# Attention with an exponential feature map, then a gated FFN: the numerator of batch 0 scaled inside its PSUM bank and divided from there on VectorE, in a new order of the whole program

## The chip, the cores and the metric

The kernel runs on one core of a Trainium2 chip. The metric is the device time of one execution in microseconds (us), measured from outside the program; each figure below is a median of several executions, or one execution taken with the hardware profiler.

The engines are named as the profile names them: PE is TensorE's matmuls and PEld its weight loads, DVE is VectorE, ACT is ScalarE, POOL is GpSimd, SP is SyncE, which only issues transfers here.

## The reference

```python
batch, n_heads, seq, head_dim, d_feat = 8, 8, 576, 64, 128
n_tokens, d_model, d_ff = 4608, 512, 1536

def phi(x):
    proj = einsum('bhsd,df->bhsf', x, w_phi)
    proj = proj - max(abs(proj), axis=-1, keepdims=True)
    return concatenate([exp(proj), exp(-proj)], axis=-1)

q_p, k_p = phi(q), phi(k)
kv  = einsum('bhsf,bhsd->bhfd', k_p, v)
z   = sum(k_p, axis=2)
num = einsum('bhsf,bhfd->bhsd', q_p, kv)
den = einsum('bhsf,bhf->bhs', q_p, z)[..., None] + 1e-06
x   = (num / den).transpose(0, 2, 1, 3).reshape(4608, 512)
out = (maximum(x @ w_gate, 0) * (x @ w_val)) @ w_out
```

So for each batch and head there is a sum over tokens (kv, with z as one more column), then for each token a numerator and a denominator, then a division. Behind the attention stands a feed-forward network (FFN) over all 4608 tokens.

## The kernel before

**Tiles.** A batch's 576 tokens are split into 512 (four tiles of 128) and 64. The 512 go through the FFN with their batch, as groups 0 to 7; the 64 of each batch are collected into a ninth group, number 8. PSUM is used as eight banks of 128 x 512 float32, which every step names itself.

**The order.** The whole program is a list of words, the string ORDER: some thousands of steps, each written as `name.arguments:banks@buffers`. A loop at the end of the kernel calls the function `do_<name>` for each word in turn, and so every engine gets its instructions in the order of the list. Nothing else schedules. An instruction waits where the data it reads, the bank that it writes or the buffer that it reuses isn't free yet, and everything behind it on its engine waits too.

**The attention of a batch.** `k3`, `k0` and their like project k with w_phi (L668, L592); `ke` takes exponentials of the projection into kp on ScalarE (L688); `kx` takes the maxima on VectorE (L696); `kk` makes factors from these; `vs`, `vq` and `vo` multiply v by the factors, mostly on GpSimd; `kv` sums over the tokens (L794), and `kc` or `kd` copies the sum out of PSUM, on ScalarE or VectorE. For q, `qe` takes exponentials into qp (L869), `qx`, `qy`, `qz` and `qu` find the maxima, and `qw` makes from them cq, the factor exp(2 max) of a token and head (L910).

**The numerator.** For each token the feature map has two halves, s = 0 and s = 1; their maximum is taken out of the exponent by scaling half 1 with cq, and the rest cancels in the division. The eight heads are dealt into three banks (GROUPS = 2, 3 and 3 heads). For each tile i of 128 tokens and each group g of heads:

- `nu` (L917, TensorE): for each head two matmuls, half 0 and half 1, side by side in the bank, 65 columns each (64 of the numerator and, as the last, the denominator).
- `nt` (L938, VectorE): t = half 1 x cq, from PSUM to a buffer; 130 or 195 elements in a row.
- `nv` (L948, VectorE): u = half 0 + t, from PSUM and the buffer.
- once for the tile, `nr` (L956, VectorE): r = 1 / (denominator), eight numbers in a row.
- once for the tile, `nx` (L960, GpSimd): xu = u x r, 512 elements in a row, to bfloat16.

```python
nc.vector.tensor_tensor(t_of(3 * serial(b, i) + g)[:, 0:n], parts(bk, n)[:, :, 1],          # nt
    scales(b, i)[:, lo:hi][:, :, None].to_broadcast([P, n, E]), op=ALU.mult)
nc.vector.tensor_tensor(u_of(serial(b, i))[:, lo:hi], parts(bk, n)[:, :, 0],                # nv
    t_of(3 * serial(b, i) + g)[:, 0:n], op=ALU.add)
nc.vector.reciprocal(r_of(serial(b, i)), u_of(serial(b, i))[:, :, D : D + 1])               # nr
eng.tensor_tensor(xu_of(n).rearrange("p (h d) -> p h d", d=D), u_of(n)[:, :, 0:D],          # nx
    r_of(n).to_broadcast([P, H, D]), op=ALU.mult)
```

xu must be transposed before the FFN. In batch 0 this is done by TensorE (`xp`, L997, into PSUM) and a copy on ScalarE (`xa`, L1011) or VectorE (`xc`, L1005); in the other batches by a transposing DMA (`xt`).

**The FFN.** Group 0 is computed in pieces of 128 tokens by four slices of the hidden layer (`pv` and `pg`, L1224: 16 matmuls of 128 columns each). Groups 1 to 6 take a hidden slice of 128 for all 512 tokens (`fv` and `fg`, L1097: four matmuls of 512 columns). The product x @ w_val is copied out of PSUM as val, by ScalarE (`va`, L1112; `pa` in group 0) or VectorE (`vb`, L1115); then VectorE takes relu(gate) x val in one instruction (`ga`, L1118). The multiplication by w_out (`fw`, L1361) uses seven products of half-size blocks instead of eight; their sums of inputs are made on GpSimd (`ps`, L1337). Groups 7 and 8 are paired in a similar scheme (`fi`, L1194).

**Dummies.** `zz.n` issues n matmuls on a tile of zeros (L455), whose results nobody reads; there are 85 in all, nearly all of them before the first FFN matmul.

## Time and profile before

| | |
|---|---|
| time, median of 3 runs | 360.83 us (359.58, 360.83, 360.85) |
| the profiled execution's own time | 360.87 us |
| its span in the profile | 359.1 us |
| instructions in the profile | 10076 |
| first FFN matmul of group 0 (L1224) starts | 28.67 us |
| matmuls on zeros (L455) | 85 |
| nt (L938) with cq, 64 of 195 and 32 of 130 elements, busy | 21.8 + 8.9 us |
| nv (L948), 72 of 195 and 36 of 130 elements, busy | 24.3 + 9.9 us |
| nx (L960) on GpSimd, 36, busy | 37.4 us |

The profile is one execution, taken by the hardware profiler. Its span runs from the first to the last instruction, and the execution's own time lies 1.8 us above it. A row such as `L938 DVE TENSOR_TENSOR t<-bank,cq 128x195 f32<-128x195 f32 x64 | 21.8, 348 | ...` is a group of instructions: line of the code, engine, operation, what is written from what, the shapes and types, how many; then the busy time in us and the mean of one in ns; then the idle time of the engine just ahead of them and what ended it. A row of the timeline has the start in us, the busy time in us, the engine, and the instructions that follow each other there. The names of buffers stand without their numbers.

### The profile page before, as it was taken

The page shows a single profiled execution, that of the slowest core. Times are in us where ns is not written, and L with a number is a line of the kernel's source. Part 1 is how long each engine was busy: PE and PEld are TensorE (multiplying, and loading weights), DVE is VectorE, ACT ScalarE, POOL GpSimd, SP SyncE. Part 2 cuts the span into 40 slices and gives each one's busy share as a digit, 9 for nine tenths or more (in the row PEclk, how much of TensorE's full clock was granted, in tenths as well). Part 3 has the DMA queues.
Part 4 walks back from the last instruction along what each step waited for, and adds up shares of the span by engine and source line. Part 5 has one row for each costly group of instructions (what it writes and reads, how often), then busy time and mean ns, then how long its engine had stood idle before and what let it go on. Part 6 is the DMA issues. An engine that isn't in the chain of part 4 may idle for free.

```text
span 359.1 us, 10076 instructions
## 1 busy us (share of the span) xinstructions
PE 352.9 (98%) x3876; PEld 222.2 (62%) x3876; DVE 312.9 (87%) x721; ACT 235.8 (66%) x564; POOL 325.6 (91%) x393
## 2 busy tenths in 40 slices
PE   8999999999999999999999999999999999999996
PEld 6678966445575656765576546666656566444684
DVE  5999999989999999999997999999898853898744
ACT  3999996986698869786897269656861424454310
POOL 8674988999999999976999589989999999999994
PEclk9999999999999999999999999999999999999999
DMA  7999999990947494369215980778300221600017
GB/s 124 257 198 204 164 199 159 180 164 7 178 68 157 53 157 95 68 127 135 58 39 105 158 136 2 176 107 103 62 0 16 45 59 25 227 0 2 0 31 206
DMA packets 90770, 38.16 MB, mean 106 GB/s; under 512 B 64226, under 2 KB 86370, under 8 KB 90722
## 3 DMA queue, kind: packets, MB, share of 16 engines
q0 software_dynamic: 33504, 15.03, 32.5%
q1 hardware_dynamic: 56754, 21.83, 27.7%
q10 hardware_dynamic: 464, 0.66, 0.8%
q8 instruction: 30, 0.49, 0.6%
q14 instruction: 18, 0.15, 0.1%
HBM read 37.81 MB, written 9.44 MB: 132 GB/s over the span
## 4 chain that ended last, share of the span: by engine, by line
PE 85%; DVE 8%; ACT 2%; DMA 2%; issue 1%; POOL 1%; SPq 0%; DVEq 0%
PE bank L1097 35%; PE bank L1361 18%; PE bank L1194 10%; PE bank L794 5%; PE bank L1224 4%; PE bank L917 3%; PE bank L592 2%; PE bank L854 2%; PE bank L1256 2%; ACT kp L688 2%; DMA w64f<-in_w_phi_dram 2%; DVE t L938 1%; DVE u L948 1%; DVE h L1118 1%; DVE mk L696 1%
## 5 line engine op out<-in xcount | busy, mean ns | idle before, releaser
L688 ACT ACTIVATE kp<-bank 128x384 bf16<-128x384 f32 x192 | 84.2, 513 | 16.6 <-DVE mk L696 7.4
L1097 PE MATMUL bank<-xTs,wv 128*128 128x512 bf16 x304 | 75.7, 379 | 0.0
L1097 PE MATMUL bank<-xTs,wg 128*128 128x512 bf16 x304 | 74.6, 379 | 0.0
L869 ACT ACTIVATE qp<-bank 128x512 bf16<-128x512 f32 x128 | 69.9, 627 | 6.5 <-PE bank L854 4.2
L1118 DVE SCALAR_TENSOR_TENSOR h<-bank,val 128x512 bf16<-128x512 f32 x90 | 60.5, 680 | 6.7 <-PE bank L1097 4.5
L1112 ACT CAST val<-bank 128x512 bf16<-128x512 f32 x59 | 35.1, 594 | 33.4 <-PE bank L1097 30.4
L745 POOL TENSOR_TENSOR vs<-vn,ek 128x780 bf16<-128x780 f32 (+2 forms) x40 | 53.8, 1366 | 0.8 <-ACT ek L705 0.4
L696 DVE TENSOR_REDUCE mk<-bank 128x3 f32<-128x384 f32 x96 | 49.1, 542 | 0.2
L960 POOL TENSOR_TENSOR xu<-u,r 128x512 bf16<-128x512 f32 x36 | 37.4, 1045 | 11.6 <-DVE r L956 11.5
L1361 PEld LDWEIGHTS <-h 128*128 128x128 bf16 x432 | 41.1, 98 | 10.0 <-issue 2.6
L1097 PEld LDWEIGHTS <-wg 128*128 128x128 bf16 x304 | 27.8, 98 | 30.2 <-issue 1.3
L1097 PEld LDWEIGHTS <-wv 128*128 128x128 bf16 x304 | 27.6, 98 | 27.3 <-issue 0.9
L877 DVE TRANSPOSE_TENSOR_REDUCE maxq<-bank 128x16 f32<-128x512 f32 x56 | 36.9, 690 | 0.1
L948 DVE TENSOR_TENSOR u<-bank,t 128x195 f32<-128x195 f32 (+1 forms) x108 | 32.9, 327 | 1.8 <-POOL xu L960 0.9
L1361 PE MATMUL bank<-wo,h 128*128 128x256 bf16 x260 | 32.5, 273 | 0.0
L1337 POOL TENSOR_TENSOR vs<-h 128x256 bf16<-128x256 bf16 x42 | 28.0, 671 | 3.7 <-DVE h L1118 3.6
L938 DVE TENSOR_TENSOR t<-bank,cq 128x195 f32<-128x195 f32 (+1 forms) x96 | 29.6, 326 | 1.9 <-PE bank L917 1.2
L917 PEld LDWEIGHTS <-qp 128*128 128x128 bf16 x512 | 23.1, 98 | 10.2 <-issue 0.5
L1337 POOL TENSOR_TENSOR h<-h,vs 128x256 bf16<-128x256 bf16 x44 | 28.6, 676 | 0.0
L1337 POOL TENSOR_TENSOR vs<-vs,h 128x256 bf16<-128x256 bf16 x42 | 28.0, 672 | 0.6
L1337 POOL TENSOR_TENSOR h<-h 128x256 bf16<-128x256 bf16 x42 | 27.9, 674 | 0.3
L917 PE MATMUL bank<-kv,qp 128*128 128x65 bf16 x512 | 26.0, 193 | 0.2 <-ACT kv L805 0.2
(156 smaller groups left out, 686.0 us busy)
## 6 DMA issues: line engine op xcount, KB each, us to landing
vn<-in_v_dram SPq DMA_DIRECT2D x24, 256.0 KB, 4.3
out_dram<-xTs SPq DMA_DIRECT2D x17, 256.0 KB, 3.0
kn<-in_k_dram POOLq DMA_DIRECT2D x7, 512.0 KB, 8.1
qn<-in_q_dram POOLq DMA_DIRECT2D x7, 512.0 KB, 8.0
out_dram<-obp SPq DMA_DIRECT2D x14, 256.0 KB, 2.6
wv<-in_moe_w_val_dram POOLq DMA_DIRECT2D x3, 512.0 KB, 9.4
wg<-in_moe_w_gate_dram POOLq DMA_DIRECT2D x3, 512.0 KB, 8.8
wo<-in_moe_w_out_dram POOLq DMA_DIRECT2D x3, 512.0 KB, 8.3
```

Source lines behind the costliest of these rows:

```text
L688: nc.scalar.activation(kp_of(3 * b + j)[:, i, s].rearrange("p n f -> p (n f)"), bank[bk[0]][:, 0 : 3 * F], AF.Exp, scale=(1.0, -1.0)[s],)
L696: nc.vector.tensor_reduce(mk_of(3 * b + j)[:, :, i], bank[bk[0]][:, 0 : 3 * F].rearrange("p (n f) -> p n f", f=F), axis=AX.X, op=ALU.max, ...
L745: nc.gpsimd.tensor_tensor(vs_of(3 * b + j)[:, s, 0:n].rearrange("p n i e -> p (n i) e")[:, :, 0:e], src[:, lo:hi].rearrange("p h i e -> p ...
L869: nc.scalar.activation(qp_of(4 * b + i)[:, s, 4 * hq : 4 * hq + 4].rearrange("p h m -> p (h m)"), bank[bk[0]], AF.Exp, scale=(1.0, -1.0)[s],)
L877: nc.vector.tensor_reduce((maxq0[:, i] if b == 0 else maxq)[:, :, i, 4 * hq : 4 * hq + 4].rearrange("p t h -> p h t"), bank[bk[0]].rearran ...
L917: nc.tensor.matmul(bank[bk[0]][:, E * n : E * (n + 1)], lhsT=qp_of(4 * b + i)[:, s, h, :], rhs=kv_of(b)[:, h, s, 0:E],)
L948: nc.vector.tensor_tensor(u_of(serial(b, i))[:, lo:hi], parts(bk, n)[:, :, 0], t_of(3 * serial(b, i) + g)[:, 0:n], op=ALU.add,)
L960: eng.tensor_tensor(xu_of(n).rearrange("p (h d) -> p h d", d=D), u_of(n)[:, :, 0:D], r_of(n).to_broadcast([P, H, D]), op=ALU.mult,)
L1097: nc.tensor.matmul(bank[bk[0]], lhsT=w[:, dc, P * f : P * f + P], rhs=xT(g)[:, dc, :], start=(dc == 0), stop=(dc == NDC - 1),)
L1118: nc.vector.scalar_tensor_tensor(h2_of(g, f), bank[bk[0]], 0.0, val_of(NFC * g + f), op0=ALU.max, op1=ALU.mult)
L1337: eng.tensor_tensor(sum_of(g, n, j), a, b, op=op)
L1361: nc.tensor.matmul(bank[bk[0]][:, col : col + HN], lhsT=x[:, P * u : P * (u + 1)], rhs=w, start=(n in (1, 5, 6) and u == us[0] and j == 0) ...
```

## The change

For the four tiles of batch 0 the steps `nu`, `nt`, `nv`, `nr` and `nx` are replaced by four new ones. The heads are dealt into two banks of four (HALVES), and each bank holds 260 columns in a row:

- `bu.0.i.g.s` (TensorE): four matmuls of 65 columns, one for each head of half g, for one half s of the features. Half s = 1 is computed first and starts the bank; s = 0 is added to it later by accumulation in PSUM.
- `bt.0.i.g` (VectorE), between the two: the bank's 260 columns are multiplied by cq in place.
- `br.0.i.g` (VectorE): reciprocals of the four denominators, read from the bank.
- `bx.0.i.g` (VectorE): xu = bank x r, 256 elements in a row, read from the bank.

12 `nu`, 12 `nt`, 12 `nv`, 4 `nr` and 4 `nx` go, and 16 `bu`, 8 `bt`, 8 `br` and 8 `bx` come; the 64 matmuls are the same in number and size. The other batches keep the old steps. Four more steps go from VectorE to ScalarE as copies of val (59 become 63, 17 become 13), and the last transposed tile of batch 0 is copied by ScalarE (`xa.0.3` for `xc.0.3`); of the copies of kv, two go over to VectorE and two to ScalarE.

ORDER is written anew from the first line to the last, with other banks and buffers. The transfers keep nearly their order. The dummies remain 85 in all. The functions that the diff adds beside these (`do_bm`, `do_fa`, `do_fb`, `do_yq`, `do_zq`, `do_z2`, `do_yr`, `do_zr`, `do_y5`, `do_y6`) are called by no word of ORDER, and `SEEDED` is empty, so that `do_fw` computes what it did.

The diff, cut to its core (two lines stand for the table ORDER, once of before and once of after):

```diff
 ORDER = """
...
-wl.1.1 kc.0.1:4 nu.0.0.0:1 nt.0.0.0:1@t0 zz.1:0 nu.0.0.2:5 qw.0.1 qx.0.1.2:2 qe.0.0.2.0:6
+bu.0.0.0.1:6 bu.0.0.1.1:7 qz.0.3:0@my2 bt.0.0.0:6 qy.0.2:2 qz.0.2:2@my0 bu.0.1.1.1:1 bu.0.1.0.1:0
...
 """
...
+    HALVES = ((0, 4), (4, 8))
...
+    def do_bu(bk, b, i, g, s):
+        lo, hi = HALVES[g]
+        for h in range(lo, hi):
+            n = h - lo
+            nc.tensor.matmul(
+                bank[bk[0]][:, E * n : E * (n + 1)],
+                lhsT=qp_of(4 * b + i)[:, s, h, :],
+                rhs=kv_of(b)[:, h, s, 0:E],
+                start=(s == 1 and h == lo),
+                stop=(h == hi - 1),
+                skip_group_check=(s == 0),
+            )
+
+    def part(bk, g):
+        lo, hi = HALVES[g]
+        return bank[bk[0]][:, 0 : E * (hi - lo)].rearrange("p (h e) -> p h e", e=E)
+
+    def do_bt(bk, b, i, g):
+        lo, hi = HALVES[g]
+        nc.vector.tensor_tensor(
+            part(bk, g),
+            part(bk, g),
+            scales(b, i)[:, lo:hi][:, :, None].to_broadcast([P, hi - lo, E]),
+            op=ALU.mult,
+        )
+
+    def do_br(bk, b, i, g):
+        lo, hi = HALVES[g]
+        nc.vector.reciprocal(r_of(serial(b, i))[:, lo:hi], part(bk, g)[:, :, D : D + 1])
+
+    def do_bx(bk, b, i, g):
+        n, (lo, hi) = serial(b, i), HALVES[g]
+        nc.vector.tensor_tensor(
+            xu_of(n).rearrange("p (h d) -> p h d", d=D)[:, lo:hi],
+            part(bk, g)[:, :, 0:D],
+            r_of(n)[:, lo:hi].to_broadcast([P, hi - lo, D]),
+            op=ALU.mult,
+        )
+
...
+    SEEDED = ()
+        firsts = (1, 5) if g in SEEDED else (1, 5, 6)
-                    start=(n in (1, 5, 6) and u == us[0] and j == 0),
+                    start=(n in firsts and u == us[0] and j == 0),
-                    skip_group_check=(n in (2, 3, 4, 7)),
+                    skip_group_check=(n not in firsts),
```

One line is added above most of the code, so a step that stood at L917 stands at L918 in the changed kernel, and those behind the new functions stand 40 lines lower and more.

What this makes of the order is seen on three engines. First TensorE's queue at the start of the program, behind the two groups of transposes of k (xTm, L645), before the change. bank_63 to bank_70 are the eight banks, `zero` is the tile of the dummies, kT the transposed k, w the projection's weights; the rows of the two dummies shown stand six times there:

```order
L645 MATMUL bank_65<-identf,xTm 128x128 x3
L455 LDWEIGHTS zero
L455 MATMUL bank_66<-zero 128x256
...
L668 LDWEIGHTS kT_77
L668 MATMUL bank_67<-w_155,kT_77 128x128
L668 LDWEIGHTS kT_77
L668 MATMUL bank_68<-w_155,kT_77 128x128
...
L410 LDWEIGHTS sel
L410 MATMUL bank_69<-w_155,sel 128x128
```

The same place after the change; the row with bank_66 stands six times, that with bank_67 four times, bank_68 once and bank_69 twice:

```order
L646 MATMUL bank_65<-identf,xTm 128x128 x3
L456 LDWEIGHTS zero
L456 MATMUL bank_66<-zero 128x256
...
L456 MATMUL bank_67<-zero 128x256
...
L456 MATMUL bank_68<-zero 128x256
L456 LDWEIGHTS zero
L456 MATMUL bank_69<-zero 128x256
...
L669 LDWEIGHTS kT_77
L669 MATMUL bank_70<-w_155,kT_77 128x128
L669 LDWEIGHTS kT_77
L669 MATMUL bank_63<-w_155,kT_77 128x128
```

Seven more dummies stand ahead of the first projection (13 for 6), and the small matmuls of L410 have left this place.

Second, VectorE's queue where the first two tiles of batch 0 are made, before the change (h, my and mz belong to the maxima of q):

```order
L938 TENSOR_TENSOR t_123<-bank_64,cq_115 128x130
L877 TENSOR_REDUCE h_152<-bank_65 128x4x4
L948 TENSOR_TENSOR u_127<-bank_64,t_123 128x130
L938 TENSOR_TENSOR t_124<-bank_63,cq_115 128x195
L938 TENSOR_TENSOR t_125<-bank_68,cq_115 128x195
L948 TENSOR_TENSOR u_127<-bank_63,t_124 128x195
L948 TENSOR_TENSOR u_127<-bank_68,t_125 128x195
L938 TENSOR_TENSOR t_126<-bank_69,cq_115 128x130
L956 RECIPROCAL r_130<-u_127 128x8
```

The same place after the change:

```order
L1008 TENSOR_TENSOR bank_69<-bank_69,cq_115 128x260
L896 TENSOR_REDUCE my_117<-bank_65 128x32
L1008 TENSOR_TENSOR bank_63<-bank_63,cq_115 128x260
L1008 TENSOR_TENSOR bank_64<-bank_64,cq_115 128x260
L904 STREAM_TRANSPOSE mz_122<-my_117 128x32
L1008 TENSOR_TENSOR bank_70<-bank_70,cq_115 128x260
L1017 RECIPROCAL r_130<-bank_64 128x4
L1017 RECIPROCAL r_131<-bank_69 128x4
L1017 RECIPROCAL r_130<-bank_63 128x4
L1021 TENSOR_TENSOR xu_133<-bank_64,r_130 128x256
L1021 TENSOR_TENSOR xu_133<-bank_63,r_130 128x256
```

The first tile's division has come over from GpSimd and stands here, behind the scalings of two tiles.

Third, ScalarE's queue up to the first copy of a transposed tile (xTs), before the change:

```order
L869 ACTIVATE qp_113<-bank_65 128x512
L869 ACTIVATE qp_112<-bank_70 128x512
L910 ACTIVATE cq_115<-mz_122 128x8
L688 ACTIVATE kp_84<-bank_68 128x384
L1011 COPY xTs<-bank_70 128x4x128
```

and after it:

```order
L870 ACTIVATE qp_113<-bank_66 128x512
L870 ACTIVATE qp_112<-bank_67 128x512
L911 ACTIVATE cq_115<-mz_122 128x8
L689 ACTIVATE kp_84<-bank_66 128x384 x2
L1051 COPY xTs<-bank_63 128x4x128
L1051 COPY xTs<-bank_69 128x4x128
```

Two exponentials of the next batch's k, for one, stand ahead of that copy, and the second tile's copy follows at once.

567 lines of the change are left out of this document (303 added, 264 removed).

## The prediction

> **What bounds the kernel now.** I read the page first, then the chain of waits, then TensorE's own waits, and then the busy time by stage, because a share over the whole span mixes stages with different limits.
>
> ```profile
> PE 352.9 (98%) x3876; PEld 222.2 (62%) x3876; DVE 312.9 (87%) x721; ACT 235.8 (66%) x564; POOL 325.6 (91%) x393
> ...
> PE 85%; DVE 8%; ACT 2%; DMA 2%; issue 1%; POOL 1%; SPq 0%; DVEq 0%
> PE bank L455 <- DVE zero L441: 1.1, 1, 1.1
> PE bank L1361 <- POOL vs L1337: 0.4, 2, 0.2
> ```
>
> TensorE is busy for 98% of the span, holds 85% of the chain that ended last, and in its list of waits hardly anything exceeds 0.2 us. So the kernel ends when TensorE has got through its queue, and a change helps only where TensorE idles or runs dummy matmuls (L455, 85 of them, which multiply zeros). The stages say which engine is beside it:
>
> ```profile
> 7.00:28.00 21.00, 20.41 (x292) 14.07 (x292) 20.71 (x54) 20.25 (x54) 15.19 (x17) 1.00 1.28 218
> 28.00:60.00 32.00, 31.80 (x532) 24.71 (x532) 31.66 (x79) 28.71 (x73) 25.43 (x30) 1.00 1.21 182
> 60.00:76.00 16.00, 15.95 (x163) 7.52 (x162) 15.94 (x41) 14.98 (x40) 15.76 (x14) 1.00 1.33 190
> 242.00:300.00 58.00, 57.58 (x561) 35.93 (x560) 46.22 (x105) 28.28 (x67) 56.92 (x71) 1.00 0.28 48
> 300.00:355.50 55.50, 55.50 (x352) 34.00 (x350) 39.24 (x63) 20.45 (x37) 53.77 (x70) 1.00 0.22 64
> ```
>
> The columns are the stretch, its length, then PE, PEld, DVE, ACT, POOL. From 7 to 76 us VectorE is busy 68.31 of 69.00 us: it never rests. From 7 to 28 ScalarE hardly rests either (20.25 of 21.00). From 242 us on VectorE has room, and GpSimd is the one that is nearly full. So there are three stages: a head (to 28.67 us) in which VectorE and ScalarE prepare batch 0 and TensorE fills time with dummies; a stretch to 76 us in which TensorE and VectorE are both full; and the rest, TensorE with GpSimd close behind. The change sits in the first stage.
>
> **How the head ends.** This is the path to the first real FFN matmul, at 28.67 us:
>
> ```profile
> 26.23 0.18 DVE L956 RECIPROCAL r<-u 128x8 f32<-128x8 f32 x1
> ...
> 26.51 1.03 POOL L960 TENSOR_TENSOR xu<-u,r 128x512 bf16<-128x512 f32 x1 [2.51 <-DVE r L956]
> ...
> 27.60 0.40 PE L997 MATMUL bank<-ident,xu 128*128 128x128 bf16 x4
> ...
> 28.03 0.59 ACT L1011 COPY xTs<-bank 128x512 bf16<-128x512 bf16 x1 [0.16 <-PE bank L997]
> ...
> 28.67 1.00 PE L1224 MATMUL bank<-xTs,wv 128*128 128x128 bf16 x15 [0.20 <-ACT xTs L1011]
> ```
>
> Reciprocal, GpSimd's division, transpose, ScalarE's copy, FFN. Before 28.67 lie all dummies; behind it TensorE is full. So the end of the program moves by as much as this point moves, plus or minus what TensorE idles later.
>
> **The numerator itself.**
>
> ```profile
> L938 DVE TENSOR_TENSOR t<-bank,cq 128x195 f32<-128x195 f32 x64 | 21.8, 348 | 1.6 <-PE bank L917 1.1 <-ACT cq L910 0.3
> L938 DVE TENSOR_TENSOR t<-bank,cq 128x130 f32<-128x130 f32 x32 | 8.9, 282 | 0.3 <-PE bank L917 0.2
> L948 DVE TENSOR_TENSOR u<-bank,t 128x195 f32<-128x195 f32 x72 | 24.3, 352 | 0.7
> L948 DVE TENSOR_TENSOR u<-bank,t 128x130 f32<-128x130 f32 x36 | 9.9, 278 | 1.1 <-POOL xu L960 0.9
> L956 DVE RECIPROCAL r<-u 128x8 f32<-128x8 f32 x36 | 6.7, 189 | 0.2
> L960 POOL TENSOR_TENSOR xu<-u,r 128x512 bf16<-128x512 f32 x36 | 37.4, 1045 | 11.6 <-DVE r L956 11.5
> L1392 DVE TENSOR_TENSOR xTs<-bank,xTs 128x256 f32<-128x256 f32 x4 | 1.7, 424 | 0.5 <-PE bank L1361 0.2
> L1216 DVE TENSOR_TENSOR val<-bank,u 128x512 bf16<-128x512 f32 x24 | 15.8, 684 | 4.6 <-PE bank L1194 3.4 <-ACT u L1210 1.2
> L1005 DVE COPY xTs<-bank 128x512 bf16<-128x512 bf16 x1 | 0.4, 384 | 0.0
> L1115 DVE CAST val<-bank 128x512 bf16<-128x512 f32 x17 | 11.4, 677 | 1.6 <-PE bank L1097 1.6
> ```
>
> Removed on VectorE, for four tiles: 8 x (348 + 352) + 4 x (282 + 278) + 4 x 189 = 8.6 us. Removed on GpSimd: 4 x 1045 = 4.2 us. Added on VectorE: 8 scalings of 260 elements in place, 8 reciprocals of 4, 8 divisions of 256. From 130 to 195 elements the row grows by 66 ns, so 260 come to 348 + 66 = 414 ns; the division is like the 256-wide row, 424; the reciprocal stays at 189. That is 8 x 1027 = 8.2 us. **VectorE saves only 0.4 us**: the addition goes to TensorE's accumulation, but the division comes over from GpSimd. No row shows a VectorE operation from PSUM to PSUM. Its bounds are the 130-wide row (282) and the 512-wide one (684), thus 8.2 - 1.1 and 8.2 + 2.2 us; I take 414, by the nearest rows. TensorE's work is unchanged: 64 matmuls of 65 columns either way, and 85 dummies either way. The old division leaves nothing late on GpSimd, which was idle 2.51 us before it.
>
> [...]
>
> Two other moves take work from VectorE in the full stretch: the last transposed tile is copied by ScalarE (384 ns less), and of the val copies two leave it and one joins before 76 us (677 ns less). With the numerator that is 0.4 + 0.4 + 0.7 = 1.5 us of VectorE's 68.3.
>
> **The start is later.** The rows of the new order show 13 dummies, not 6, between the two first transposes and the first projection.
>
> ```profile
> 1.06 3.38 PE L455 MATMUL bank<-zero 128*128 128x256 bf16 x15 [1.06 <-DVE zero L441]
> 4.23 1.49 PE L645 MATMUL bank<-identf,xTm 128*128 128x128 f32 x6
> 5.51 1.49 PE L455 MATMUL bank<-zero 128*128 128x256 bf16 x6
> 7.10 0.34 PE L668 MATMUL bank<-w,kT 64*128 64x128 bf16 x6
> 7.46 0.49 ACT L688 ACTIVATE kp<-bank 128x384 bf16<-128x384 f32 x1 [1.86 <-PE bank L668]
> 8.06 0.50 PE L455 MATMUL bank<-zero 128*128 128x256 bf16 x3
> 8.40 0.50 PE L614 MATMUL bank<-ident,kn 128*128 128x128 bf16 x6
> 11.56 1.92 ACT kp L688 x5
> ```
>
> A dummy takes (4.23 - 1.06) / 15 = 0.21 us at first and (8.40 - 8.06) / 3 = 0.11 us at 8 us, so TensorE doubles its pace in between. Six from 5.51 end at 6.8; seven more end at 7.6 (at 0.11) to 8.3 (at 0.21). The projection, at 7.10 now, then starts at 7.6 or later. ScalarE's first exponential, 0.36 us behind its projection now, moreover reads the second projection (0.1 to 0.2 us on), so it starts near 8.2 rather than 7.46. ScalarE then has the same queue up to the first copy plus one exponential (26, not 25; 1.92 / 5 = 0.38 us). With nothing gained inside, the copy would fall 0.74 + 0.38 = 1.1 us later; the old queue has some 0.3 us of idle to give. **I take +0.8 us for the first FFN matmul** (bounds 0, if VectorE's shorter path through the division and a better packing eat it up, and +1.7, if the dummies all run slowly).
>
> [...]
>
> **What comes back later.** (a) In the stretch to 76 us VectorE holds TensorE up only in fractions. Of the 1.5 us less I count 0.5 us as a gain (bounds 0 and 1.5). (b) Between operations on the whole array and those on 32-row strips TensorE loses a moment:
>
> ```profile
> 127.13 1.03 PE L1097 MATMUL bank<-xTs,wv 128*128 128x512 bf16 x4
> 128.00 0.34 PE L917 MATMUL bank<-kv,qp 128*128 128x65 bf16 x6
> 129.17 1.03 PE L1097 MATMUL bank<-xTs,wg 128*128 128x512 bf16 x4
> 130.12 0.52 PE L592 MATMUL bank<-w,kT 32*128 32x128 bf16 x24
> ```
>
> Four FFN matmuls take 0.87 us before an ordinary group, 0.95 before a strip group. The new order has 50 such changes, the old one 55: 5 x 0.08 = 0.4 us (bounds 0 and 0.5). (c) Near the end TensorE waits for GpSimd's sums:
>
> ```profile
> 290.56 1.16 POOL L1169 TENSOR_TENSOR qT<-xTs 128x512 bf16<-128x512 bf16 x1 [0.68 <-DMA xTs<-xu]
> 292.40 1.48 PE L1361 MATMUL bank<-wo,vs 128*128 128x256 bf16 x12 [0.22 <-POOL vs L1337]
> 295.39 0.83 PE L1361 MATMUL bank<-kp,vs 128*128 128x256 bf16 x6 [0.20 <-POOL vs L1337]
> ```
>
> Behind 290.56 GpSimd does not stop again, and ends 1.4 us before TensorE. It has 4.2 us less to do, but 83 rather than 82 operations behind this place, so I credit these two waits, 0.4 us (bounds 0.8 gained, 0.6 lost). (d) Two dummies now stand in the second stage, inside a time when TensorE is full: 0.1 us lost (0 to 0.2).
>
> **Sum.** The profiled execution took 360.87 us, 359.1 of it span; the median of the three runs is 360.83, the same. +0.8 - 0.5 - 0.4 - 0.4 + 0.1 = -0.4, so **360.4 us** with rounding. A measurement of this kernel can tell about 0.5%, 1.8 us, from no change: below 359.0 is faster, over 362.6 slower.
>
> **Rivals.** *Faster*: VectorE, not TensorE, sets the pace from 7 to 76 us. Then its 1.5 us count in full, and with the GpSimd waits (0.8) and the strip changes (0.5), and a head that is no later, the time is 360.87 - 2.8 = 358.1. For it: 68.31 of 69.00 us busy. Against it: TensorE is just as full from 28 us on. *Slower*: the in-place scaling costs 684 ns, not 414, in the stage in which VectorE has no rest: 8 x 0.27 = 2.2 us, thus 360.4 + 2.2 = 362.6, and with the dummies at the slow pace (another 0.5 or more) 363.2. It decides from about 680 ns. Against it: every row here grows by about 1 ns per element, whatever it reads. *No effect*: the change removes waiting that TensorE doesn't have; the order merely deals the same work out anew, 360.9. For it: 85% of the chain is TensorE, and its work is equal.
>
> **Chances.** Forecast 0.45, no effect 0.13, faster 0.24, slower 0.18. The first two lie within 0.5%. The range, 358.4 to 362.9, takes in nearly all of the faster and the slower case, the likeliest alone being 359.4 to 361.6.
>
> **What would show it.** Right: first FFN matmul near 29.5 us, the first exponential near 8.2, the scaling near 0.41 us, no wait of TensorE over 0.3 us behind 30 us, GpSimd not waiting for VectorE's reciprocal in the head. Wrong: a first FFN matmul before 28.5 us, scalings over 0.6 us, or TensorE idle for over 1 us in all behind 30 us.

## The result, and the profile after

The changed kernel takes **368.73 us** (median of 4 runs, 368.45 to 369.26), the kernel before 360.25 us beside it: a ratio of **1.0232** (95% interval 1.0217 to 1.0248). That is slower by 8.4 us, and outside the range of the prediction. The profiled execution took 368.56 us, its span 366.8 us; that of before took 360.87 and 359.1.

First the page of the changed kernel, the busy time and the chain of work that ended last:

```profile
PE 353.4 (96%) x3876; PEld 223.5 (61%) x3876; DVE 313.9 (86%) x712; ACT 237.7 (65%) x569; POOL 320.7 (87%) x389
PE 70%; POOL 8%; DVE 7%; ACT 6%; DMA 4%; issue 3%; SPq 1%; POOLq 0%; DVEq 0%; ACTq 0%
```

TensorE was 85% of the chain and is 70%; GpSimd, which was 1%, is 8%. TensorE's waits in the changed kernel (what waits, for whom; us in all, times, the longest) show where a good part of that went:

```profile
PE bank L411 <- DVE sel L404: 2.8, 1, 2.8
PE bank L456 <- ACT kp L689: 1.1, 1, 1.1
...
PE bank L993 <- DVE bank L1008: 0.7, 1, 0.7
PE bank L795 <- POOL vs L746: 0.6, 1, 0.6
PE bank L1417 <- POOL h L1392: 0.5, 1, 0.5
```

Before, none of these waits was there. The 1.1 us are dummies (L456) that wait for a bank at 19.23 us. The 2.8 us are two small matmuls (`w1`, L411) that wait for `sel`, a selection matrix that VectorE copies out of the identity. The timeline of the changed kernel at that place, start and duration in us:

```profile
20.57 2.91 POOL L746 TENSOR_TENSOR vs<-vn,ek 128x768 bf16<-128x768 f32 x2
21.55 2.09 DVE L404 COPY sel<-ident 64x256 bf16<-64x256 bf16 x1
23.70 0.39 PE L411 MATMUL bank<-w,sel 64*128 64x128 bf16 x2 [2.78 <-DVE sel L404]
...
24.29 0.43 PE L795 MATMUL bank<-vs,kp 128*128 128x65 bf16 x4
24.58 0.41 PE L795 MATMUL bank<-vs,kp 128*128 128x65 bf16 x4
...
27.45 0.28 PE L795 MATMUL bank<-vs,kp 128*128 128x65 bf16 x4
...
33.63 0.55 PE L1279 MATMUL bank<-xTs,wv 128*128 128x128 bf16 x7
```

The same copy in the timeline of the kernel before:

```profile
6.86 0.32 DVE L403 COPY sel<-ident 64x256 bf16<-64x256 bf16 x1
```

Three things are to be seen. The copy takes 2.09 us rather than 0.32, and it ends (23.64) 0.16 us behind the end of GpSimd's two multiplications (23.48), which had begun ahead of it. TensorE stands still meanwhile. And the matmuls that come next, the sums kv, run at 0.29 us a group at first and at 0.15 us from 27 us on. The busy time of that stretch (length, PE, PEld, DVE, ACT, POOL, then the granted clock) in the changed kernel says why:

```profile
24.00:28.00 4.00, 4.00 (x83) 3.93 (x83) 3.75 (x8) 3.31 (x8) 2.65 (x4) 0.63 0.85 106
```

The granted clock is 0.63, where the same stretch before had 1.00. So TensorE looks busy for 4.00 us and gets less done in them. That the idle 2.8 us cost it its clock for the next 3 us is tested below (`fill`).

The difference of the two profiled executions can be laid out by three marks: the first FFN matmul with gate weights, the end of the last matmul, and the execution's own time.

| | before | after | difference |
|---|---|---|---|
| first FFN matmul (value) | 28.67 | 33.63 | +4.96 |
| first FFN matmul (gate) | 33.17 | 38.03 | +4.86 |
| from there to the end of the last matmul | 322.34 | 323.72 | +1.38 |
| from there to the end of the span | 3.58 | 5.03 | +1.45 |
| own time | 360.87 | 368.56 | +7.69 |

So the head is late by 4.9 us, 1.4 us are lost over the next 320 us, and another 1.45 us go after TensorE has finished. Of the 1.4 us, about 1.0 can be read as waits: over this stretch TensorE's list has 1.6 us in the changed kernel and 0.6 before.

### The profile page after: what moved, and what is told of

It is laid out like the page before. It is cut to its first block, busy times and chain, and to the rows that moved or that the text cites. A ratio compares the mean times of both kernels' runs of the same rounds, so it can differ in the third digit from the quotient of the medians.

```text
span 366.8 us, 10082 instructions
## 1 busy us (share of the span) xinstructions
PE 353.4 (96%) x3876; PEld 223.5 (61%) x3876; DVE 313.9 (86%) x712; ACT 237.7 (65%) x569; POOL 320.7 (87%) x389
## 4 chain that ended last, share of the span: by engine, by line
PE 70%; POOL 8%; DVE 7%; ACT 6%; DMA 4%; issue 3%; SPq 1%; POOLq 0%; DVEq 0%; ACTq 0%
PE bank L1151 27%; PE bank L1417 17%; PE bank L1249 10%; PE bank L795 4%; PE bank L1279 4%; ACT kp L689 4%; POOL vs L746 3%; PE bank L918 2%; PE bank L593 2%; PE bank L855 2%; ACT qp L870 1%; DMA vm<-in_v_dram 1%; DMA vn<-in_v_dram 1%; DMA km<-in_k_dram 1%; POOL vs L1392 1%
## 5 line engine op out<-in xcount | busy, mean ns | idle before, releaser
L689 ACT ACTIVATE kp<-bank 128x384 bf16<-128x384 f32 x192 | 82.1, 518 | 15.3 <-PE bank L593 9.8
L1151 PE MATMUL bank<-xTs,wg 128*128 128x512 bf16 x304 | 75.6, 379 | 0.0
L1166 ACT CAST val<-bank 128x512 bf16<-128x512 f32 x63 | 36.9, 597 | 43.7 <-PE bank L1151 39.0
L961 POOL TENSOR_TENSOR xu<-u,r 128x512 bf16<-128x512 f32 x32 | 33.1, 1038 | 10.0 <-DVE r L957 8.7
L949 DVE TENSOR_TENSOR u<-bank,t 128x195 f32<-128x195 f32 (+1 forms) x96 | 29.9, 330 | 1.5
L939 DVE TENSOR_TENSOR t<-bank,cq 128x195 f32<-128x195 f32 (+1 forms) x84 | 25.6, 328 | 2.6 <-ACT cq L911 0.8
L795 PEld LDWEIGHTS <-kp 128*128 128x128 bf16 x640 | 23.2, 100 | 4.5 <-issue 0.7
L918 PEld LDWEIGHTS <-qp 128*128 128x128 bf16 x448 | 19.3, 97 | 8.2 <-issue 0.4
```

The source lines that it names most:

```text
L689: nc.scalar.activation(kp_of(3 * b + j)[:, i, s].rearrange("p n f -> p (n f)"), bank[bk[0]][:, 0 : 3 * F], AF.Exp, scale=(1.0, -1.0)[s],)
L795: nc.tensor.matmul(out_ps[:, h - lo, s, :], lhsT=lhsT, rhs=rhs, start=(at == 0), stop=(at == 2 * n * (C + 1) - 1),)
L1151: nc.tensor.matmul(bank[bk[0]], lhsT=w[:, dc, P * f : P * f + P], rhs=xT(g)[:, dc, :], start=(dc == 0), stop=(dc == NDC - 1),)
L1166: nc.scalar.copy(val_of(NFC * g + f), bank[bk[0]])
```

## The experiments

### The late copy

**`sl_early`**: the changed kernel, with the copy back near its old place, everything else left.

```diff
-... sl ...                 (in the list where batch 0's sums begin)
+kg.1:2@kT0 sl              (behind the first transposes of k)
```

> The changed kernel with one step moved: the copy that makes sel (VectorE, 64 x 256, bf16 from SBUF to SBUF) stands again at the start of the program, where VectorE idles from 6.8 to 7.9 us; the two matmuls that read it stay where they are. Theory A (the copy is held up by GpSimd's multiplications, which run from 20.57 to 23.48 us, and TensorE waits for it): the copy takes 0.32 us, TensorE's wait of 2.8 us for sel goes, its clock stays at 1.00 between 24 and 28 us, and the first FFN matmul comes at 30.0 to 30.8 instead of 33.63; 365.2 to 365.9 us in all. Theory B (GpSimd's multiplications for the first batch are late in themselves, 20.57 to 23.48 for 18.13 to 21.04 before, and the sums over the tokens wait for them anyway): the wait moves to GpSimd, the first FFN matmul stays behind 32.5, and the time within 1 us of 368.7.

367.14 us (ratio 1.0193, interval 1.0161 to 1.0225). TensorE's wait of 2.8 us for the copy is gone, the clock in 24 to 28 us is 1.00, and the first FFN matmul starts at 30.39 us, 3.2 us earlier. But the time falls by 1.6 us only. The list of TensorE's waits of this kernel shows one that wasn't there:

```profile
PE bank L1268 <- DMA wg<-in_moe_w_gate_dram: 2.3, 1, 2.3
```

This list is that of the longest execution, 369.03 us; the other three took 366.43 to 367.40, so that the wait may well be shorter in them. The mechanism of the head was right; what it is worth was not. The transfer of the gate weights comes next.

**`sl_reduce`**: the copy stays where the change put it, but is written as two reductions over an axis of length 1, each for one half of sel.

```diff
-nc.vector.tensor_copy(sel..., ident...)
+for a in range(2):
+    nc.vector.tensor_reduce(sel[:, a]..., ident...[:, a][:, None, :, None]..., axis=AX.X, op=ALU.max)
```

> The changed kernel with sel made at the same place, by VectorE, from the same tile, but with two reductions over an axis of length 1 in place of the copy. Theory A1 (it is this form of instruction, a copy from SBUF to SBUF, that cannot run beside GpSimd): the two take 0.2 to 0.3 us each, and the time is that of the kernel with the early copy plus at most 0.5 us. Theory A2 (anything that VectorE runs there from SBUF to SBUF is held up while GpSimd is busy): they end at 23.5 us or later, and the time stays at 368.7.

366.78 us (1.0177, 1.0156 to 1.0197). From the timeline of this kernel:

```profile
20.44 2.91 POOL L738 TENSOR_TENSOR vs<-vn,ek 128x768 bf16<-128x768 f32 x2
21.42 0.45 DVE L394 TENSOR_REDUCE sel<-ident 64x128 bf16<-64x128 bf16 x2
30.90 1.95 PE L1271 MATMUL bank<-xTs,wv 128*128 128x128 bf16 x32
```

GpSimd's multiplications run at the same time as in the changed kernel and as long, and yet the reductions are through in 0.45 us. So it isn't the place alone, and not VectorE's queue: it is this copy, as an operation, that has to wait for GpSimd. Beside the same work it takes 2.09 us, against 0.45 for the two reductions; why it waits and they don't, no run shows.

**`late_sl`**: the kernel before, with the copy moved late.

```diff
-... kT0 sl ... w1:6 ... wa:6 ...
+vp.0:0 sl ... kv.0.1:4 w1:3 ... kc.0.1:4 wa:3
```

> The kernel before, with the copy that makes sel moved from 6.9 us to where VectorE stands at 19.2 us, while GpSimd multiplies v (18.13 to 21.04); the two matmuls that read it follow behind the sums over the tokens, and their copy behind those of kv. Theory A (a copy from SBUF to SBUF on VectorE stands still until GpSimd pauses): it takes 2.0 to 2.3 us instead of 0.32, everything behind it on VectorE is 1.7 to 2.0 us late in the stage in which VectorE never rests, and the time rises by 1.0 to 1.9 us to 361.3 to 362.3. Theory Z (the copy in the changed kernel was slow for a reason of its own order): 0.3 to 0.4 us, and 360.2 to 360.8.

361.53 us (1.003, 1.0017 to 1.0042). The timeline of this kernel:

```profile
17.95 2.95 POOL L734 TENSOR_TENSOR vs<-vn,ek 128x768 bf16<-128x768 f32 x2 [0.41 <-DMA vn<-in_v_dram]
18.62 0.95 DVE L392 COPY sel<-ident 64x256 bf16<-64x256 bf16 x1
```

The copy is blocked in the old order too, but for 0.95 us and not for the 2 us expected: it came in behind the first of the two multiplications (17.95 + 1.47 = 19.42 us; the copy ends at 19.57). In the changed kernel it had to wait for both. What decides between these two cases stayed open. TensorE's list shows no wait for sel here. Still the time rose by 1.0 us, as much as theory A had put down to a copy of 2 us; what carried it was not taken apart.

**`fill`**: the changed kernel with 24 more dummies ahead of the two small matmuls, so that TensorE keeps its clock while it waits.

```diff
-w1:6
+zz.24:6 w1:6
```

> The changed kernel with 24 more matmuls on zeros ahead of the two that wait for sel, which cover TensorE's wait of 2.8 us with work that nobody needs. Theory C (TensorE's low clock from 24 to 28 us, 0.63, comes from its own idle time before): the copy still takes 2.1 us, the clock stays at 1.00, the 80 matmuls of the sums over the tokens take 2.6 instead of 3.9 us, and the time falls by 1.0 to 1.4 us to 367.3 to 367.7. Theory D (the clock is set by something else there, or the slow matmuls are hidden behind ScalarE): no change, 368.4 to 369.0.

369.34 us (1.025, 1.0231 to 1.0269). The copy takes as long as before, and the clock is 1.00 in this stretch (row of the busy times of this kernel):

```profile
24.00:28.00 4.00, 4.00 (x97) 3.38 (x96) 3.66 (x9) 3.58 (x10) 2.44 (x4) 1.00 0.78 100
```

The first FFN matmul comes 1.0 us earlier (32.64), so the low clock was the result of the idle wait: 0.63 behind an idle time of 2.8 us, 1.00 where dummies fill it. The total did not fall: this step of the theory was wrong. The profile of `fill` shows a wait for a transposed tile that the changed kernel doesn't have, and it is longer than what the head had gained:

```profile
PE bank L1239 <- DMA xTm<-xu: 1.2, 1, 1.2
```

Whether the other executions have this wait isn't known.

### The end of the program

**`no_out8`**: the changed kernel without the last two steps that write out from the ninth group on SyncE's queue, four transfers of 128 KB; this part of the output is left out.

```diff
-ow.8.3 ... ow.8.2
```

> The changed kernel without four of the output transfers of group 8 (the two steps of 128 KB x 2 on SP's queue ahead of the last ones), so that this part of the output is not written. The span now ends 5.05 us behind TensorE's last matmul, before it ended 3.59 us behind it. Theory E (the last transfers wait for those ahead of them, since the output of group 8 is ready 7 us later than before): the last transfer lands 2.2 us after its issue instead of 3.6, and the time falls by 1.2 to 1.6 us to 367.1 to 367.5. Theory F (the tail is longer for another reason, such as the last addition on VectorE): within 0.4 us of 368.7.

366.88 us (1.019, 1.0149 to 1.0231). The span ends 3.54 us behind the last matmul, not 5.03.

**`tail`**: nothing left out; one transfer of group 7 moved ahead of them.

```diff
-ow.8.3 ... oq.7.0.0
+oq.7.0.0 ow.8.3
```

> The changed kernel with one transfer (256 KB of the output of group 7, ready at 352 us) taken out from behind two steps of group 8's output on SP's queue, which wait for VectorE until 355.9 and 357.2, and put ahead of them. Theory E (the transfers of the last 5 us wait for each other): the last transfer lands 0.5 to 1.0 us earlier behind TensorE's last matmul (span end 4.1 to 4.6 behind it for 5.05), and the time is 367.7 to 368.2 for 368.7. Theory F (it is the number of transfers behind 357 us on the two queues, whose issue takes its time, not their bytes): tail of 4.9 to 5.1 us, and 368.4 to 369.0.

367.10 us (1.0194, 1.0163 to 1.0226), and 3.65 us behind the last matmul: the gain of 1.6 us was larger than expected. The queue of SyncE at the end, in the changed kernel:

```profile
355.96 2.48 SPq L1511 DMA_DIRECT2D out_dram<-obp  x4
358.54 3.07 SPq L1515 DMA_DIRECT2D out_dram<-xTs  x3
361.70 0.90 SPq L1507 DMA_DIRECT2D out_dram<-xTs  x1
```

and in `tail`:

```profile
351.66 0.39 SPq L1504 DMA_DIRECT2D out_dram<-xTs  x1
355.65 2.50 SPq L1500 DMA_DIRECT2D out_dram<-obp  x4
359.65 1.62 SPq L1504 DMA_DIRECT2D out_dram<-xTs  x2
361.37 0.45 SPq L1496 DMA_DIRECT2D out_dram<-xTs  x1
```

The transfers from obp wait for VectorE until 355.96 us, and in the changed kernel everything behind them waits too. Then all of them come close together at the very end: the last transfer on ScalarE's queue (out from xTs, 128 KB) takes 3.6 us from issue to landing after, 2.2 us before and 2.2 us in `tail`.

**`fix2`**: the reductions and the moved transfer together.

```diff
-nc.vector.tensor_copy(sel..., ident...)
+nc.vector.tensor_reduce(...)  (twice)
-ow.8.3 ... oq.7.0.0
+oq.7.0.0 ow.8.3
```

> The changed kernel with both mends that worked alone: sel made by two reductions (366.8 alone), and the transfer of group 7 ahead of group 8's two (367.1 alone). If the two losses are separate, as theories A and E have it, their gains add up: 1.9 + 1.6 us, thus 365.0 to 365.6. If the second is hidden behind the first or the other way round: 366.2 or more.

365.54 us (1.0146, 1.0124 to 1.0167), as expected: the two mends add up to 3.2 us. By the ratio some 5.2 us are left.

### The new numerator by itself

**`numer_before`**: the order before, with batch 0's numerator in the new form.

```diff
-nu.0.0.0:1 nt.0.0.0:1@t0 ... nv.0.0.0:1@u0 ... nr.0.0@r0 ... nx.0.0@xu0
+bu.0.0.0.1:1 bt.0.0.0:1 ... bu.0.0.0.0:1 ... br.0.0.0:1@r0 bx.0.0.0:1@xu0 (and so on)
```

> The kernel before, with batch 0's numerator alone in the new form: in the old order of the program, the 44 steps of the four tiles give way to the 40 new ones at the same places (VectorE's divisions right behind the reciprocals), and a few steps beside them take another bank. The copies of val, of kv and of the last tile stay as they were. Theory N (the numerator as the prediction priced it: 0.4 us less on VectorE, the first tile's GpSimd division of 1.03 us off the path, TensorE's matmuls unchanged): first FFN matmul at 27.9 to 28.7 us, and 359.6 to 360.6 us in all. Theory P (the chain of matmul, scaling, matmul, reciprocal and division inside one bank makes TensorE wait, as the 0.7 us for VectorE's scaling in the changed kernel): first FFN matmul behind 29.2, and 361.3 us or more.

363.65 us (1.0085, 1.0066 to 1.0104): +3.1 us. TensorE's waits of this kernel, and VectorE's operations in it:

```profile
PE bank L982 <- DVE bank L997: 2.5, 7, 0.5
...
L997 DVE TENSOR_TENSOR bank<-bank,cq 128x260 f32<-128x260 f32 x8 | 3.3, 424 | 1.1 <-PE bank L982 0.6 <-ACT kp L678 0.5
```

Half 1 has to be computed, then scaled, and only then can half 0 be added. Seven times TensorE stands still for VectorE, and VectorE for TensorE: its busy time in 23.5 to 36 us is 10.78 of 12.50 us, where before it was 12.48.

**`numer2`** puts other work of TensorE between the halves. **`numer3`** takes some of it out again, so that VectorE waits less for the second halves, and gives VectorE a maximum of k to do meanwhile.

```diff
-bu.0.1.1.0:3 zz.5:5 kr.1.1:1265
+zz.5:5 xp.0.0:0 kr.1.1:1265 bu.0.1.1.0:3     (numer2; tiles 2 and 3 likewise)
```

```diff
-kr.1.1:1265 bu.0.1.1.0:3 ... pv.0.1:3 bu.0.3.0.0:0 bu.0.3.1.0:4
+bu.0.1.1.0:3 kr.1.1:1265 ... bu.0.3.0.0:0 bu.0.3.1.0:4 pv.0.1:3     (numer3, on numer2)
```

> The kernel before with batch 0's numerator in the new form, as in the earlier trial, but with other work put between the two matmul halves of a bank on TensorE's queue: the dummies and the projection of batch 1 stand ahead of the second halves of tile 1, the first FFN matmuls ahead of those of tiles 2 and 3, and the first tile is transposed and copied as soon as VectorE has divided it. Theory P1 (the loss of 3.1 us in the earlier trial was TensorE waiting in place, 2.5 us in 7 waits, since the second half stood right behind the scaling that it needs): the waits fall below 0.8 us, the first FFN matmul comes at 28.0 to 28.8, and the time is 359.8 to 361.0. Theory P2 (the form itself costs, since every bank goes through four turns between two engines): 361.8 us or more, wherever the second halves stand.

> The kernel before with the new numerator as in the second trial (363.13), and VectorE's queue ordered so that it seldom waits for TensorE's second halves: those of tile 1 stand ahead of the projection, those of tile 3 ahead of an FFN matmul, and a maximum of k between scaling and reciprocal. VectorE idles 1.35 us between 23.5 and 36 us in the second trial, 0.02 in the kernel before. Theory X (the loss of 2.5 us is VectorE's waiting for TensorE between the turns): idle time under 0.9 us, and 362.0 to 362.7. Theory Y (it is something else in the form, such as banks that are held longer): 363.0 or more.

363.13 us (1.0069, 1.0053 to 1.0086) and 362.71 us (1.0058, 1.0043 to 1.0073). The waits for a scaling fall to 0.9 us, VectorE is busy for 11.15 and 11.68 us of the 12.50, but losses of 2.5 and 2.1 us remain. So the turns are part of the cost in the old order, and what the rest of it is stays open. The saving that the new form was credited with was not found in any arrangement tried.

**`ny_before`**: the kernel before, with nothing of the new form but the division on VectorE.

```diff
-nx.0.0@xu0 ... nx.0.3@xu3
+ny.0.0@xu0 ... ny.0.3@xu3
```

> The kernel before with one thing changed: the division of batch 0's four tiles is done by VectorE instead of GpSimd, at the same places, on the same 512 elements from the buffer u; nothing else moves. GpSimd's 4 x 1.05 us go, VectorE gets 4 x 0.6 to 0.75 us. Theory V (in the stage up to 36 us VectorE sets the pace, since it never rests there, and what it gets more comes out at the end): 362.2 to 363.4 us for 360.6. Theory W (TensorE sets the pace, and the shorter division, 0.7 us for 1.05, helps the path to the first FFN matmul): 360.0 to 360.9.

362.77 us (1.0067, 1.0047 to 1.0087). Four divisions of 690 ns on VectorE, 2.8 us, cost 2.4 us (by the ratio; 1.7 to 3.1). From the list of waits of this kernel:

```profile
PE bank L986 <- DVE xu L949: 1.9, 3, 0.8
```

In the old order VectorE's added work in the head comes out in the time nearly in full. The first FFN matmul doesn't show it: it starts at 28.65 us, as before. The first gate matmul does, at 34.75 us for 33.17.

**`relief`**: the kernel before, with work taken from VectorE instead: the last transposed tile and three copies of val go to ScalarE, as in the change.

```diff
-xc.0.3:5 ... vb.1.3:4@val3 ... vb.1.4:4@val2 ... vb.1.1:5@val2
+xa.0.3:5 ... va.1.3:4@val3 ... va.1.4:4@val2 ... va.1.1:5@val2
```

> The kernel before with four copies moved from VectorE to ScalarE, as the change does with copies of its kind: the last transposed tile of batch 0 (0.38 us, at 38 us) and three copies of val of group 1 (0.68 us each, from 73 us on). Theory V (VectorE sets the pace until about 76 us): 0.3 to 0.8 us faster, 359.8 to 360.3. Theory W (TensorE sets it, or ScalarE has no room either): within 0.3 us of 360.6.

361.03 us (1.0005, 0.9987 to 1.0023): nothing gained.

**`zz7`**: the kernel before with seven more dummies ahead of the first projection, 13 as in the change.

```diff
-zz.6:3
+zz.6:3 zz.7:3
```

> The kernel before with seven more dummies ahead of the first projection, 13 instead of 6 as in the changed kernel, and 92 in all. The prediction's step: the projection starts 0.4 to 0.8 us later (7.5 to 7.9), ScalarE's first exponential as much, and the first FFN matmul 0.4 to 0.8 behind 28.67; 360.9 to 361.4 us. The other view: the chain to the first FFN matmul has 0.3 us or more of slack behind the first exponential, so that it moves by under 0.2 us, and the time by nothing.

360.70 us (1.0008, 0.9994 to 1.0022). The timeline of this kernel shows the 13 dummies and the projection behind them:

```profile
5.53 1.67 PE L444 MATMUL bank<-zero 128*128 128x256 bf16 x13
7.13 0.34 PE L657 MATMUL bank<-w,kT 64*128 64x128 bf16 x6
```

The projection starts at 7.13, before at 7.10 us, and the first FFN matmul at 28.72 us. In the kernel before the projection had waited for its weights, which VectorE finished at 7.04 us; in this execution the dummies ended when the projection began. When the weights come is not the same everywhere either: in the changed kernel they were there at 6.35 us. So the rows of one execution don't say how much the dummies delay the projection; the time says that it costs nothing here.

### What is left in the new order

**`pool_early`** (on `sl_reduce`) lets GpSimd start its multiplications vs earlier; **`fix3`** (on `fix2`) moves work of batch 1 on GpSimd and VectorE forward; **`fix4`** joins `pool_early` and `tail` and moves further factors forward.

```diff
-kk.0.1.0@ek0 ... kk.0.1.1 ... lq.1.2 ... vs.0.1.0
+kk.0.1.0@ek0 kk.0.1.1 ... vs.0.1.0 lq.1.2     (pool_early)
```

```diff
-kk.1.1.0@ek2 ... kk.1.1.1 ... vs.1.1.1@vs3 ... vs.1.1.0 ... vo.1.1
+kk.1.1.0@ek2 kk.1.1.1 ... lv.1.0 lv.1.1 vs.1.1.1@vs3 vs.1.1.0 vo.1.1     (fix3)
```

```diff
-kx.0.2.0:4 ... kx.0.2.2:1 ... ke.0.2.3.1:5 ... kk.0.2.1@ek1 ... kk.0.2.0
+kx.0.2.0:4 kx.0.2.2:1 ... ke.0.2.3.1:5 kk.0.2.1@ek1 kk.0.2.0     (fix4)
```

> The kernel with sel made by the two reductions, and two steps moved further: ScalarE makes the second factor of k of the first group right behind the first one (it stands behind five exponentials), and GpSimd issues the load of q for batch 1 behind its first two multiplications and not ahead of them, where it waits 4.9 us for TensorE to free the buffer. Theory G (GpSimd's multiplications, which start at 16.9 us for 14.0 before, now set when the sums over the tokens end and when the weights of the gate are loaded): they start at 13.7 to 14.5, TensorE's wait of 1.1 us for them goes, the first FFN matmul comes at 29.3 to 30.3 instead of 30.90, and the time is 365.0 to 366.2 for 366.8. Theory H (VectorE's maxima of q set it): the first FFN matmul within 0.3 of 30.90, and 366.4 to 367.2.

> The kernel with both mends, and GpSimd's first two multiplications for batch 1 brought forward: the factor that they need is made by ScalarE right behind its twin (it stands 3.9 us behind it), and four issues of loads that stand ahead of them on GpSimd go behind them. Theory Q (GpSimd, which idles 11 to 13 us from 26.4 us on and starts on batch 1 at 45 us for 40.8 before, is late from there on, and TensorE waits for it at 85 us, 1.3 us, and later): these multiplications start at 41 to 42 us, the wait at 85 us falls below 0.5, and the time is 0.5 to 1.2 us under that with both mends. Theory R (it is the loads behind them that matter, or GpSimd makes up for it): within 0.4 us.

> The changed kernel with both mends (365.5), with the two steps of GpSimd's queue and ScalarE's from the trial on GpSimd's start, and with the two factors of the third group of heads made by ScalarE right behind the maxima (at 17 us; they stand behind five exponentials of q, 19.0 and 21.1). In the trial on GpSimd's start, GpSimd began 2.5 us earlier but waited for these factors, and ended no sooner, 23.1 us for 23.35. Theory S (ScalarE's order of the factors sets GpSimd's end, and with it the sums over the tokens): GpSimd's multiplications of this batch end at 20.9 to 21.7, TensorE's wait for them goes, the first FFN matmul comes at 29.6 to 30.4 for 31.01, and the time is 364.3 to 365.0. Theory T (VectorE's maxima of q and copies set it): first FFN matmul within 0.3 of 31.01, 365.2 or more.

367.05 us (1.0174, 1.0150 to 1.0198), 365.61 us (1.0133, 1.0109 to 1.0157) and 366.20 us (1.0143, 1.0119 to 1.0168): none differs from its base by more than its interval. In `pool_early` vs starts 2.5 us earlier than in `sl_reduce` and ends only 0.2 us earlier (23.12 us), since the last two pieces wait for ScalarE's factors ek (timeline of GpSimd in this kernel):

```profile
14.20 2.90 POOL L738 TENSOR_TENSOR vs<-vn,ek 128x768 bf16<-128x768 f32 x2
19.59 1.47 POOL L738 TENSOR_TENSOR vs<-vn,ek 128x768 bf16<-128x768 f32 x1 [0.83 <-ACT ek L698]
21.65 1.47 POOL L738 TENSOR_TENSOR vs<-vn,ek 128x768 bf16<-128x768 f32 x1 [0.59 <-ACT ek L698]
```

**`no_turn`** and **`no_scale`** (both on `fix2`) ask whether the numerator is what is left.

```diff
 def do_bt(bk, b, i, g):
-    nc.vector.tensor_tensor(part(bk, g), part(bk, g), scales(b, i)[:, lo:hi]..., op=ALU.mult)
+    nc.vector.tensor_tensor(obp..., scales(b, i)..., scales(b, i)..., op=ALU.mult)     (no_turn)
+    pass                                                                            (no_scale)
```

> On the kernel with both mends (sel by two reductions, out's last pair of transfers ahead; 365.54 us), the eight scalings of batch 0's numerator write elsewhere: a multiplication of 344 elements from cq alone, about as long, at the same places of VectorE's queue, but with no matmul ahead or behind. So half 1 of the numerator of batch 0 isn't scaled. VectorE's work stays, the turn matmul - scaling - matmul goes. Theory T (the turn is what the numerator costs in the new order too): the waits of TensorE for a scaling (0.7 us) go and the first FFN matmul comes 0.5 to 1.5 us earlier, 364.0 to 365.0 us. Theory U (what is left of the loss lies in VectorE's work or elsewhere in the order, not in the turn): 365.3 to 365.9 us.

> The same, and the eight scalings are left out altogether (half 1 of batch 0's numerator isn't scaled): VectorE has 8 x 0.42 = 3.4 us less to do in the head. Theory V (VectorE's work in the head comes out in the time): 1.5 to 2.5 us below no_turn, 362.0 to 363.5 us. Theory Z (the rest of the order sets the pace: GpSimd's and ScalarE's factors, weights that come later): within 0.5 us of no_turn.

365.72 us (1.0147, 1.0122 to 1.0171) and 364.82 us (1.0140, 1.0109 to 1.0172), beside `fix2`'s 1.0146. The stand-in of `no_turn` took 498 ns, a little longer than a scaling (422 ns in the changed kernel); VectorE is busy for 313.1 us in all, for 312.4 in `fix2`. So in the new order the turn between the engines is not what holds the program: theory T fell and theory U held. Without the scalings the median is 0.9 us under that of `no_turn`, which neither theory V nor theory Z had named, and the ratios overlap: 3.4 us of VectorE's work are worth little here. The first FFN matmul hardly moves, 31.13 us in `fix2` and in `no_turn` and 31.07 in `no_scale`, for 28.67 before. And it is late already where the numerator begins, here in `fix2` and in the kernel before:

```profile
26.21 0.49 PE L985 MATMUL bank<-kv,qp 128*128 128x65 bf16 x8
23.46 0.29 PE L917 MATMUL bank<-kv,qp 128*128 128x65 bf16 x4
```

The 2.75 us between these two rows are as much as the whole lateness of the head in `fix2`. They arise ahead of the new steps: the sums over the tokens end 1.6 us later (25.25 us for 23.62), and 1.1 us more pass before the numerator's first matmul. No run isolates the step that makes them. In `no_scale`, with the scalings gone, TensorE waits behind the numerator's start for ScalarE's exponentials of q:

```profile
PE bank L585 <- ACT qp L862: 0.6, 2, 0.3
```

The rows of the first gate matmul show a second bound close behind. First its row in `fix2`, and the issue of the last piece of those weights on GpSimd's queue:

```profile
25.91 0.76 POOL L551 DMA_DIRECT2D wg<-in_moe_w_gate_dram  x1
35.87 1.07 PE L1271 MATMUL bank<-xTs,wg 128*128 128x128 bf16 x16 [0.17 <-DMA wg<-in_moe_w_gate_dram]
```

then in `no_scale`:

```profile
26.09 0.76 POOL L551 DMA_DIRECT2D wg<-in_moe_w_gate_dram  x1
38.25 1.07 PE L1265 MATMUL bank<-xTs,wg 128*128 128x128 bf16 x16 [2.61 <-DMA wg<-in_moe_w_gate_dram]
```

and in the kernel before:

```profile
23.22 0.78 POOL L558 DMA_DIRECT2D wg<-in_moe_w_gate_dram  x1
33.17 1.06 PE L1224 MATMUL bank<-xTs,wg 128*128 128x128 bf16 x16
```

The weights' transfer is issued by GpSimd, behind its multiplications vs, and these end 2.4 us later in the new order (23.48 for 21.04 us in the changed kernel). The transfer is used 10.0 us after its issue in the kernel before and in `fix2`, and 12.2 us after it in the profiled execution of `no_scale`, which took 368.17 us while the others of this kernel took 364.23 to 365.32. In no mended form does the first gate matmul start ahead of 35.8 us, 2.7 us behind the kernel before. TensorE stands still for the weights there in `sl_early` (2.26 us), `sl_reduce` (0.34), `fix2` (0.17), `no_turn` (0.68) and `no_scale`, but its lists show no such wait in `pool_early` and `fix3`. So the later issue is a bound that a sooner head would meet, and not by itself the cause of the 2.70 us: in `fix2` 2.46 of them are there at the first FFN matmul, which doesn't read these weights. What is left in `fix2` is made up thus: 2.70 us up to the first gate matmul, 1.50 behind it (359.71 - 35.87 = 323.84 us, for 322.34) and 0.2 at the end make the 4.45 us between the profiled executions, 365.32 and 360.87. A kernel in which only the issue of these weights is earlier was not run (`fix4` issued it at 24.50 us, but its first FFN matmul came at 33.0 us, for other reasons).

## Why the prediction was wrong, point by point

- **Where the change acts**: right. The head is where most is lost; the first FFN matmul came at 33.63 us, not 29.5.
- **"... the end of the program moves by as much as this point moves"**: the rest of that sentence, "plus or minus what TensorE idles later", turned out as large as the move. In `sl_early` the first FFN matmul came 3.2 us sooner and the time fell by 1.6 us; in `ny_before` it stood where it was and the time rose by 2.4 us. Behind this point the other tiles and weights of group 0 are still to come, and TensorE waits for them.
- **"The start is later ... I take +0.8 us"**: this step failed. It followed ScalarE's queue and counted dummies. The first exponential did start where it said (8.07 us for 8.2), but seven more dummies cost nothing in the old order (`zz7`; no run takes them out of the new one), and the first FFN matmul was 5 us late, almost three times the step's upper bound of 1.7, for reasons that the step doesn't hold. The step `sl`, with the two matmuls that wait for it, had been moved from 6.86 to 21.55 us, beside GpSimd's multiplications, and was priced at nothing. That is worth 1.6 to 2.0 us (`sl_early`, `sl_reduce`). A move of an instruction had been costed by its queue and not by its neighbours on the other engine. With this mended the first FFN matmul is still 2.5 us late (`fix2`), and the numerator's first matmul 2.75 us; which of the moved steps ahead of it does that stays open.
- **GpSimd's relief**: "the old division leaves nothing late on GpSimd" was right, and worthless. Its multiplications vs end 2.4 us later in the new order, and with them the issue of the gate weights, the bound that a sooner head meets. Behind that GpSimd waits 13.2 us at a stretch for batch 1's transposed k. The waits at 292 and 295 us did go, but others came, and the long stretch lost 1.4 us where the sum had credited 0.4 for them.
- **The numerator's price**: right in size. The rows of the changed kernel give 422 ns for a scaling and 406 for a division, and 171 ns for a reciprocal, together 8.0 us where 8.2 was predicted.

```profile
L1008 DVE TENSOR_TENSOR bank<-bank,cq 128x260 f32<-128x260 f32 x8 | 3.2, 422 | 0.1
L1017 DVE RECIPROCAL r<-bank 128x4 f32<-128x4 f32 x8 | 1.3, 171 | 0.0
L1021 DVE TENSOR_TENSOR xu<-bank,r 128x256 bf16<-128x256 f32 x8 | 3.0, 406 | 0.0
```

  The reciprocals from PSUM took 171 ns for 4 numbers, beside 189 ns for 8 from SBUF in the kernel before. What the sum missed is that the form makes two engines take turns: in the old order the new form cost 2 to 3 us (`numer_before`, `numer2`, `numer3`), and 2.5 us of waits for a scaling stand in the first of these. In the new order taking the turns away gained nothing (`no_turn`).
- **VectorE's 1.5 us less, "I count 0.5 us"**: wrong at these places. In the old order work added to VectorE in the head costs nearly its whole length (`ny_before`, 2.4 of 2.8 us), and work taken off it later is worth nothing (`relief`). The average over 7 to 76 us hid this difference. In the new order even 3.4 us taken off in the head gained about 0.9 by the medians (`no_scale`).
- **The end**: not looked at. The prediction took the end of TensorE's queue for the end of the program; 1.4 to 1.6 us were lost behind it (`tail`).
- **The rivals**: the slower one named a scaling of 684 ns. It was 422, so its mechanism was wrong although its sign was right. The faster one, with VectorE as the pace, was half right as a mechanism, for the old order's head, and pointed the other way. The third, no effect, fell with the measured time.
- **The strip changes (0.4 us) and the two dummies in the second stage**: not taken apart by any run. Counted over the rows of the two timelines, matmuls on 32-row strips and others follow each other 78 times before and 78 times after, so the traces show nothing to credit.

No version tried is faster than the kernel before; the best mended form of the changed kernel is 1.3 to 1.5% slower.

## What to carry to other kernels

When an order is rewritten, look at each short instruction that changed its neighbours, and above all at copies on VectorE that now stand beside GpSimd's work, and at every transfer that an engine issues behind its own computation: these cost next to nothing in a list of durations. Here a copy of 0.32 us took 2.09 and cost 1.6 to 2.0 us of the time, and TensorE waited up to 2.6 us for weights that were issued 2.4 to 2.9 us later than before. Before an in-place step is counted as a saving, ask which engine waits at each end of it. As the mark for a stage take a point behind which nothing of the stage is still awaited; the first matmul of the FFN was not one. And follow the program to the landing of its last transfer, not to its last matmul.

## What the runs showed of the hardware that had not been expected

A copy of 64 x 256 elements on VectorE took 0.32 us alone, 0.95 us when it got in between two multiplications on GpSimd, and 2.09 us when it had to sit out both; in `late_sl` it ended 0.15 us, in the changed kernel 0.16 us behind the end of a multiplication. TensorE's granted clock fell to 0.63 over 4 us after a wait of 2.8 us, and stayed at 1.00 when dummies filled the wait. A transfer of 512 KB that was used 10.0 us after its issue in the kernel before and in `fix2` was used 12.2 us after it in one execution of `no_scale`; TensorE waited 2.6 us for it, and this execution was 3.4 us longer than the median of its kernel.
